# Gathering one unit's u with the next unit's kv and y on TensorE, from the fourth batch on

## The chip, the core and the metric

The kernel runs on one core of a Trainium2 chip. The metric is the device time of one launch in microseconds. One launch does everything below; inputs and output lie in the chip's memory.

## The reference, cut to what matters

```
# q, k, v: (8, 8, 576, 64)
q_s  = softmax(q, over the 64 columns)        k_s = softmax(k, over the 576 rows)
kv   = einsum('bhsd,bhse->bhde', k_s, v)      attn = einsum('bhsd,bhde->bhse', q_s, kv)
x    = attn as (8, 576, 512)
h    = relu(x^T @ w_tok1) @ w_tok2            # 576 -> 256 -> 576, over the rows
u    = x + h^T
out  = u + relu(u @ w_ch1) @ w_ch2            # 512 -> 1536 -> 512, over the columns
```

## The kernel before

The work has two kinds of pieces.

**Units.** A unit is one batch `b` and one pair of heads `j`; there are 8 x 4 = 32 of them, `n = 4 b + j`. A unit goes through these steps on TensorE:
- `softmax_k` holds one small product (L235, 128 columns, full fp32, two passes: "mb"), which spreads the maxima of k over the partitions.
- `stage_kv` makes kv: ten products of 65 columns in full fp32 (L277). The trace counts two passes for each, 20 rows.
- `stage_y` makes y = q_s^T w_tok1: 14 products of 256 columns (L337). Its operands are split into a high and a low part of type fp32r.
- `stage_h1` multiplies y by kv: two products of 128 columns in full fp32 (L345, four passes) and splits the result into `hh` and `hl`.
- `stage_u` makes u in two parts of 320 and 256 columns, nine fp32r products each (L381). Its results are copied into `uh` by ScalarE (L388) and `ul` by VectorE (L389).
- `stage_qT` turns q on VectorE and ScalarE (L315, L323) and splits it into `qth`, `qtl`, which `stage_u` reads. It has no product here.

**Steps.** The channel product runs over 9 groups `g` of 512 rows and 12 slices `f`. A step `(g, f)` is `ch1` (L409, 12 products of 512 columns into one `ps_h` bank, emptied by ScalarE L412 and VectorE L413 into `h2h`, `h2l`), and then `ch2` of the step before (L421, 12 products of 512 columns into the four `ps_o` banks). After a group's last `ch2`, `out_end` empties `ps_o` (L452, L453).

`todo` says where unit pieces go: an entry at `i` is issued in step `i` between its `ch1` and the `ch2`, an entry at `i + 0.5` after that `ch2`. A step is 24 products of 512 columns. `n0` = 24 is the first step of group 2; groups begin at `n0`, `n0 + 12` and so on. From the fourth batch on, unit `n` has its entries at `n0 + 12 (b - 3) + 3 j`, so that four units go with one group of 12 steps.

All pieces of later units and all `ch1` share the four `ps_h` banks, in turn. `qh`, `ql`, `qth`, `qtl`, `ys`, `hh`, `hl`, `kvh`, `kvl` have one buffer each. The order on an engine is not the order in which the code issues: a scheduler places instructions by its own estimate, within the dependences. An engine then runs its list in that order.

Of the kernel before, what the change touches and what calls it, by code (L numbers as in the profile page):

```python
# [20 lines left out]
def attn_mixer_kernel(ctx: ExitStack, tc: tile.TileContext, q, k, kt, v, wt, out, dims):  # L21
# [6 lines left out]
    NF = DCH // P  # L28
# [80 lines left out]
    def f32(ap):  # L109
        return ap.bitcast(F32)  # L110

    def split(hi, lo, src, lo_eng):

        nc.scalar.copy(hi, src)  # L114
        lo_eng.tensor_tensor(lo, src, f32(hi), op=ALU.subtract)  # L115
# [3 lines left out]
    def ps_unit(dtype=F32):  # L119

        pools = unit_banks[0]
        pool, name = pools[turn[0] % len(pools)]
        turn[0] += 1
        return pool.tile([P, 512], dtype, name=name)
# [25 lines left out]
    def load_v(n):  # L150
        if n < NU and n not in v_of:
            t = v_ring[n % 2 if n < NE else 0]
            for h in range(2):
                nc.sync.dma_start(t[:, 0:C, h, 0:D], v[n][:, 0:C, h * D : (h + 1) * D])
            nc.sync.dma_start(t[0:TL, C, :, 0:D], v[n][0:TL, C, :].rearrange("p (h d) -> p h d", h=2))
            v_of[n] = t
# [113 lines left out]
    def stage_kv(u):  # L270
        kx, vt = u["k"], v_of[u["n"]]
        kv = ps_unit()

        for c in range(C1):
            for h in range(2):
                hs = slice(h * D, (h + 1) * D)
                nc.tensor.matmul(kv[hs, 0 : D + 1], kx[:, c, hs], vt[:, c, h, :], start=(c == 0), stop=(c == C))  # L277

        if u["n"] != NE - 1:
            load_v(u["n"] + 2 if u["n"] < NE else u["n"] + 1)  # L280
        rs = sm.tile([P, 1], F32, name="rs")
        nc.vector.tensor_scalar(rs, kv[:, D : D + 1], 1e-9, None, op0=ALU.add)
        nc.vector.reciprocal(rs, rs)
        kvf = kv_ring[u["n"] % len(kv_ring)]
        for h in range(2):
            hs = slice(h * D, (h + 1) * D)
            nc.scalar.activation(kvf[hs, hs], kv[hs, 0:D], AF.Copy, scale=rs[hs])
        u["kvf"] = kvf
        if u["early"]:
            return  # L290
        kvh = wk.tile([P, P], F32R, name="kvh")
        kvl = wk.tile([P, P], F32R, name="kvl")
        split(kvh, kvl, kvf, nc.vector)
        u["kvh"], u["kvl"] = kvh, kvl

    def stage_qT(u):

        qx = u["q"]
        if u["early"]:
            qt = early.tile([P, S], F32, name="qt")  # L300
            t = ps_unit()
            for c in range(C):
                nc.tensor.transpose(t[:, c * P : (c + 1) * P], qx[:, c, :], f32(ident))
            nc.scalar.copy(qt[:, 0:S0], t)
            t = ps_unit()
            nc.tensor.transpose(t[:, 0:P], qx[:, C, :], f32(ident))
            nc.scalar.copy(qt[:, S0:S], t[:, 0:TL])
            u["qt"] = qt
            return
        qth = wk.tile([P, S], F32R, name="qth")  # L310
        qtl = wk.tile([P, S], F32R, name="qtl")
        u["qth"], u["qtl"] = qth, qtl

        turned = cv.tile([P, C1 * P], U32, name="cv_s").bitcast(F32).rearrange("p (c t) -> p c t", t=P)
        nc.vector.transpose(turned, qx)  # L315
        k = 0
        for x in range(P // Q):
            n = C1 if x * Q < TL else C
            for y in range(P // Q):
                xs, ys = slice(x * Q, (x + 1) * Q), slice(y * Q, (y + 1) * Q)  # L320
                eng = (nc.vector.tensor_copy, nc.vector.tensor_copy, nc.scalar.copy)[k % 3]
                k += 1
                eng(qx[ys, 0:n, xs], turned[xs, 0:n, ys])  # L323
        split(qth, qtl, qx.rearrange("p c t -> p (c t)")[:, 0:S], nc.vector)

    def stage_y(u):
        y = ps_unit()
        if u["early"]:
            mm = [(u["q"][:, c, :], w1f[:, c, :]) for c in range(C1)]
        else:  # L330
            qh, ql = u["qh"], u["ql"]
            mm = []
            for c in range(C):
                mm += [(qh[:, c, :], w1h[:, c, :]), (qh[:, c, :], w1l[:, c, :]), (ql[:, c, :], w1h[:, c, :])]
            mm += [(qh[:, C, :], w1th), (qh[:, C, :], w1tl)]
        for i, (a, w) in enumerate(mm):
            nc.tensor.matmul(y[:, 0:TOK], a, w, start=(i == 0), stop=(i == len(mm) - 1))  # L337
        ys = (early if u["early"] else wk).tile([P, TOK], F32, name="ys")
        nc.scalar.copy(ys, y[:, 0:TOK])
        u["y"] = ys  # L340

    def stage_h1(u):
        h1 = ps_unit()
        for n in range(NT):
            nc.tensor.matmul(  # L345
                h1[:, n * P : (n + 1) * P], u["y"][:, n * P : (n + 1) * P], u["kvf"], start=True, stop=True
            )
        pool = early if u["early"] else wk
        hh = pool.tile([P, NT, P], F32R, name="hh")
        hl = pool.tile([P, NT, P], F32R, name="hl")  # L350
        src = h1[:, 0 : NT * P].rearrange("p (n c) -> p n c", n=NT)
        nc.scalar.activation(hh, src, AF.Relu)
        nc.vector.scalar_tensor_tensor(hl, src, 0.0, f32(hh), op0=ALU.max, op1=ALU.subtract)  # L353
        u["hh"], u["hl"] = hh, hl
# [7 lines left out]
    def stage_u(u, half):  # L362
        b, j = u["b"], u["j"]
        edge = (b + 1) * CW - b * S
        cut = min(max(edge, S - 320), 320)
        n0, n1 = ((0, cut), (cut, S))[half]
        N = n1 - n0
        ns = slice(n0, n1)
        t = ps_unit()
        if u["early"]:  # L370
            mm = [(u["kvf"], u["qt"][:, ns])]
        else:
            mm = [(u["kvh"], u["qth"][:, ns]), (u["kvh"], u["qtl"][:, ns]), (u["kvl"], u["qth"][:, ns])]
        for n in range(NT):
            mm += [
                (u["hh"][:, n, :], w2h[:, n, ns]),
                (u["hh"][:, n, :], w2l[:, n, ns]),
                (u["hl"][:, n, :], w2h[:, n, ns]),
            ]
        for i, (a, w) in enumerate(mm):  # L380
            nc.tensor.matmul(t[:, 0:N], a, w, start=(i == 0), stop=(i == len(mm) - 1))  # L381
        for g, a0, a1 in ((b, n0, min(n1, edge)), (b + 1, max(n0, edge), n1)):
            if a0 < a1:
                at = b * S + a0 - g * CW
                uh, ul = (x[:, j, at : at + a1 - a0] for x in uT[g])
                src = t[:, a0 - n0 : a1 - n0]
                emptied[:] = [
                    nc.scalar.copy(uh, src).ins,  # L388
                    nc.vector.tensor_tensor(ul, src, f32(uh), op=ALU.subtract).ins,  # L389
                ]  # L390
# [66 lines left out]
    units = {}  # L457

    def begin(n):
        if n < NU and n not in units:  # L460
            units[n] = load_unit(n // NJ, n % NJ)

    def soft(n):
        if n < NU:
            softmax_k(units[n])
            softmax_q(units[n])

    def pe_stages(n):
        def s1():
            stage_qT(units[n])  # L470
            stage_kv(units[n])

        def s2():
            stage_y(units[n])

        def s3():
            stage_h1(units[n])
            stage_u(units[n], 0)

        def s4():  # L480
            stage_u(units[n], 1)

        return s1, s2, s3, s4
# [64 lines left out]
    n0 = len(steps)  # L548
# [9 lines left out]
    def put(at, fn):  # L558
        todo.setdefault(int(2 * at) / 2, []).append(fn)

    put(n0 - 12, prepare)
    for n in range(NE, NU):
        b, j = divmod(n, NJ)
        if b == 2:
            at = (n0 - 10, n0 - 9, n0 - 9, n0 - 7.5) if j == 0 else [n0 - 9.5 + 2 * j + x for x in (0, 0.5, 1, 1.5)]
        else:
            at = [n0 + (b - 3) * NF + 3 * j + x for x in (0, 1, 1.5, 2)]
        s1, s2, s3, s4 = pe_stages(n)
        put(at[0], s1)
        put(at[0], lambda n=n: soft(n + 1))  # L570
        put(at[0] + 0.5, lambda n=n: begin(n + 2))
        for x, fn in zip(at[1:], (s2, s3, s4)):
            put(x, fn)

    pend = None

# [84 lines left out]
```

## Time and profile before

| | |
|---|---|
| median of 3 runs | 822.23 us (821.69 to 822.65) |
| profiled execution | 822.09 us, of which the span of the engines is 820.3 |
| TensorE busy | 803.5 us, 98% of the span |
| VectorE, ScalarE, GpSimd busy | 490.5, 340.0, 84.4 us |
| TensorE's waits that the trace names | 10.7 us, all before 239 us |

The first 180 us prepare weights and the first two batches; units of the third batch end at 231 us. From 239 us to 682 us the 20 units of batches four to eight run among the steps, and from 682 us on only steps are left. In the timeline a row gives the start, the time, the engine, the line, the operation, and how many like it follow one another ("x2"). The times of single matrix products overlap: what one costs is the distance from its start to the next start.

### The profile page before, as it was taken

What the parts mean: (1) busy time and instruction counts of PE and PEld (TensorE: products, weight loads), DVE (VectorE), ACT (ScalarE), POOL (GpSimd) and SP (SyncE); (2) the same over time, 40 slices, a digit from 0 to 9 for tenths busy, and PEclk for the clock granted to TensorE, in tenths of its full rate; (3) what the DMA queues carried; (4) which work ended last, traced back from release to release, by engine and by line L of the source; (5) the groups of instructions that cost most, each with busy time, mean ns of one, the idle gap of its engine ahead of it and who ended that gap; (6) DMA issues with size and microseconds to landing.
All of it is one profiled execution on the core that took longest, in us unless ns stands there. A gap on an engine that the chain in (4) does not pass through costs nothing.

```text
span 820.3 us, 11946 instructions
## 1 busy us (share of the span) xinstructions
PE 803.5 (98%) x4512; PEld 678.1 (83%) x4512; DVE 490.5 (60%) x1104; ACT 340.0 (41%) x898; POOL 84.4 (10%) x69
## 2 busy tenths in 40 slices
PE   7899999989999999999999999999999999999997
PEld 6688888878888888888888888888888888888886
DVE  6999998897875455855576555845575324113112
ACT  6976564457544344443434443434443421101110
POOL 1000010102201011111111111101111100000100
PEclk9999999999999999999999999999999999999999
DMA  9753433424222112312232221312121001001001
GB/s 298 241 161 93 150 108 113 139 83 126 64 73 85 48 53 63 109 52 64 64 114 63 64 64 35 113 47 63 39 91 48 15 1 51 1 1 51 1 1 51
DMA packets 60634, 63.55 MB, mean 77 GB/s; under 512 B 40865, under 2 KB 40993, under 8 KB 60577
## 3 DMA queue, kind: packets, MB, share of 16 engines
q1 hardware_dynamic: 55392, 53.36, 22.2%
q10 hardware_dynamic: 5184, 9.44, 3.1%
q8 instruction: 35, 0.57, 0.3%
q14 instruction: 23, 0.18, 0.1%
HBM read 53.35 MB, written 9.44 MB: 77 GB/s over the span
## 4 chain that ended last, share of the span: by engine, by line
PE 89%; DVE 6%; DMA 3%; ACT 1%; SPq 1%; issue 0%; DVEq 0%; ACTq 0%
PE ps_h L409 34%; PE ps_o L421 34%; PE ps_h L381 8%; PE ps_h L337 5%; PE ps_h L277 2%; DMA stg<-in_w 2%; PE ps_h L345 1%; DMA kt_t<-in_kt 1%; PE ps_o L381 1%; PE ps_h L235 1%; PE ps_o L337 1%; DVE mc L219 1%; DVE q_t L323 1%; DVE cv_s L176 1%; DVE cv_s L181 1%; DVE stg L179 0%
## 5 line engine op out<-in xcount | busy, mean ns | idle before, releaser
L409 PE MATMUL ps_h<-uh,cw 128*128 128x512 f32 x864 | 268.6, 391 | 0.3 <-DVE cw L115 0.3
L421 PE MATMUL ps_o<-h2h,cw 128*128 128x512 f32 x864 | 250.0, 392 | 2.2 <-DVE cw L115 2.2
L421 PEld LDWEIGHTS ps_o<-h2h,cw 128*128 128x128 f32 x864 | 160.0, 188 | 34.7 <-ACT h2h L412 2.4
L409 PEld LDWEIGHTS ps_h<-uh,cw 128*128 128x128 f32 x864 | 159.3, 188 | 31.6 <-DVE cw L115 0.8
L413 DVE SCALAR_TENSOR_TENSOR h2l<-ps_h,h2h 128x512 fp32r<-128x512 f32 x108 | 74.3, 688 | 170.4 <-ACT h2h L412 170.2
L412 ACT ACTIVATE h2h<-ps_h 128x512 fp32r<-128x512 f32 x108 | 64.4, 596 | 253.8 <-PE ps_h L409 251.5
L409 PE MATMUL ps_h<-ul,cw 128*128 128x512 f32 x432 | 168.7, 390 | 0.0
L421 PE MATMUL ps_o<-h2l,cw 128*128 128x512 f32 x432 | 151.9, 394 | 0.0
L409 PEld LDWEIGHTS ps_h<-ul,cw 128*128 128x128 f32 x432 | 81.1, 188 | 17.4
L421 PEld LDWEIGHTS ps_o<-h2l,cw 128*128 128x128 f32 x432 | 79.7, 188 | 15.9
L323 DVE COPY q_t<-cv_s 32x160 f32<-32x160 f32 (+1 forms) x264 | 62.1, 235 | 45.2 <-POOL ql L115 41.9
L237 POOL TENSOR_TENSOR k_t<-k_t,mb 128x640 f32<-128x640 f32 x24 | 38.0, 1583 | 350.6 <-ACT mb L236 350.6
L115 POOL TENSOR_TENSOR ql<-q_t,qh 128x640 fp32r<-128x640 f32 x24 | 39.2, 1633 | 220.7 <-ACT qh L114 218.2
L245 DVE TENSOR_REDUCE st<-q_t 128x10 f32<-128x640 f32 x32 | 26.2, 817 | 38.2 <-DMA q_t<-in_q 38.2
L323 ACT COPY q_t<-cv_s 32x128 f32<-32x128 f32 (+1 forms) x120 | 36.8, 307 | 2.1 <-DVE cv_s L315 0.7
L256 ACT ACTIVATE q_t<-q_t 128x640 f32<-128x640 f32 x24 | 17.7, 739 | 40.4 <-DVE q_t L255 40.4
L381 PE MATMUL ps_h<-w2h,hh 128*128 128x256 f32 (+1 forms) x112 | 32.6, 299 | 0.0
L381 PE MATMUL ps_h<-w2l,hh 128*128 128x256 f32 (+1 forms) x112 | 32.6, 296 | 0.0
L389 DVE TENSOR_TENSOR ul<-ps_h,uh 128x320 fp32r<-128x320 f32 (+4 forms) x76 | 26.8, 372 | 7.4 <-ACT uh L388 6.8
L388 ACT CAST uh<-ps_h 128x320 fp32r<-128x320 f32 (+4 forms) x76 | 24.4, 337 | 15.6 <-PE ps_h L381 11.2
L381 PE MATMUL ps_h<-w2h,hl 128*128 128x320 f32 (+1 forms) x112 | 29.8, 300 | 0.3 <-DVE hl L353 0.2
L219 DVE TENSOR_REDUCE mc<-kt_t 128x1 f32<-128x640 f32 x32 | 25.9, 809 | 4.8 <-DMA kt_t<-in_kt 3.5
(144 smaller groups left out, 1077.8 us busy)
## 6 DMA issues: line engine op xcount, KB each, us to landing
stg<-in_w SPq DMA_DIRECT2D x28, 512.0 KB, 4.0
kt_t<-in_kt SPq DMA_DIRECT2D x32, 320.0 KB, 3.2
q_t<-in_q SPq DMA_DIRECT2D x32, 320.0 KB, 3.1
v_t<-in_v SPq DMA_DIRECT2D x64, 128.0 KB, 2.6
out<-stg ACTq DMA_DIRECT2D x32, 256.0 KB, 2.1
k_t<-in_k SPq DMA_DIRECT2D x24, 320.0 KB, 3.3
v_t<-in_v SPq DMA_DIRECT2D x32, 32.0 KB, 2.5
out<-part ACTq DMA_DIRECT2D x4, 256.0 KB, 2.3
```

The costliest lines, as they stand in the source:

```text
L115: lo_eng.tensor_tensor(lo, src, f32(hi), op=ALU.subtract)
L219: nc.vector.tensor_reduce(mc, ktt, axis=AX.X, op=ALU.max)
L237: nc.gpsimd.tensor_tensor(kx, kx, mb.unsqueeze(1).broadcast_to([P, C1, P]), op=ALU.subtract)
L245: nc.vector.tensor_reduce(st[:, 0, :], qt, axis=AX.X, op=ALU.max)
L323: eng(qx[ys, 0:n, xs], turned[xs, 0:n, ys])
L337: nc.tensor.matmul(y[:, 0:TOK], a, w, start=(i == 0), stop=(i == len(mm) - 1))
L381: nc.tensor.matmul(t[:, 0:N], a, w, start=(i == 0), stop=(i == len(mm) - 1))
L389: nc.vector.tensor_tensor(ul, src, f32(uh), op=ALU.subtract).ins,
L409: nc.tensor.matmul(t, cw[f][x][:, n, :], w, start=(i == 0), stop=(i == 3 * NJ - 1))
L412: nc.scalar.activation(hh, t, AF.Relu).ins,
L413: nc.vector.scalar_tensor_tensor(hl, t, 0.0, f32(hh), op0=ALU.max, op1=ALU.subtract).ins,
L421: nc.tensor.matmul(o, cw[f][x][:, n, :], w, start=(first and i == 0), stop=(last and i == 2))
```

## The change

Before, the entries of a unit from the fourth batch on were: qT and kv at `at`, y at `at + 1`, h1 and half of u at `at + 1.5`, the other half at `at + 2`. Now they are gathered. At `at - 1` come both halves of u of the unit before, then kv, y and qT of this unit; h1 follows at `at + 0.5`, and u of the last unit stands alone. `at - 1` is step 2, 5, 8 or 11 of a group's 12, where `at` was 0, 3, 6 or 9. The softmax of the next unit and the loads of the one after keep their places behind kv (now also behind y).

```diff
+    prev = None
     for n in range(NE, NU):
         b, j = divmod(n, NJ)
+        s1, s2, s3, s4 = pe_stages(n)
         if b == 2:
             at = (n0 - 10, n0 - 9, n0 - 9, n0 - 7.5) if j == 0 else [n0 - 9.5 + 2 * j + x for x in (0, 0.5, 1, 1.5)]
-        else:
-            at = [n0 + (b - 3) * NF + 3 * j + x for x in (0, 1, 1.5, 2)]
-        s1, s2, s3, s4 = pe_stages(n)
-        put(at[0], s1)
-        put(at[0], lambda n=n: soft(n + 1))
-        put(at[0] + 0.5, lambda n=n: begin(n + 2))
-        for x, fn in zip(at[1:], (s2, s3, s4)):
-            put(x, fn)
+            put(at[0], s1)
...
+            continue
+        at = n0 + (b - 3) * NF + 3 * j - 1
+        if prev is not None:
+            put(at, lambda n=prev: (stage_u(units[n], 0), stage_u(units[n], 1)))
+        put(at, lambda n=n: (stage_kv(units[n]), stage_y(units[n]), stage_qT(units[n])))
+        put(at, lambda n=n: soft(n + 1))
+        put(at + 0.5, lambda n=n: begin(n + 2))
+        put(at + 1.5, lambda n=n: stage_h1(units[n]))
+        prev = n
+    put(at + 3, lambda n=prev: (stage_u(units[n], 0), stage_u(units[n], 1)))
```

In the lists of instructions below, a number behind a name tells buffers apart, and "x2" stands for so many alike in a row. TensorE before, where group 3 begins and unit 16 has its kv:

```order
L421 MATMUL ps_o<-h2h_109,cw_1388 128x512 x7
L277 MATMUL ps_h<-v_t,k_t 64x65 x2
L409 MATMUL ps_h<-uh_101,cw_117 128x512 x2
L277 MATMUL ps_h<-v_t,k_t 64x65
L409 MATMUL ps_h<-ul_105,cw_117 128x512
L277 MATMUL ps_h<-v_t,k_t 64x65 x7
L235 MATMUL ps_h<-dg,ones 128x128
L421 MATMUL ps_o<-h2l_113,cw_1388 128x512 x3
L421 MATMUL ps_o<-h2h_109,cw_1388 128x512
L421 MATMUL ps_o<-h2l_113,cw_1388 128x512
L409 MATMUL ps_h<-uh_101,cw_117 128x512 x2
```

The kv products stand in three pieces, with `ch1` products (L409) of the next group between them, and mb (L235) directly behind. Four units, the first ones of the last four batches, have kv in three pieces like this; the other sixteen have it in one. TensorE now, the end of u of unit 15, kv of unit 16 and the beginning of its y:

```order
L381 MATMUL ps_h<-w2h,hh 128x256
L381 MATMUL ps_h<-w2l,hh 128x256
L381 MATMUL ps_h<-w2h,hl 128x256
L277 MATMUL ps_h<-v_t,k_t 64x65 x10
L337 MATMUL ps_h<-w1h,qh 128x256
L337 MATMUL ps_h<-w1l,qh 128x256
L337 MATMUL ps_h<-w1h,ql 128x256
```

And the end of that y:

```order
L337 MATMUL ps_h<-w1h,ql 128x256
L337 MATMUL ps_h<-w1th,qh 128x256
L337 MATMUL ps_h<-w1tl,qh 128x256
L235 MATMUL ps_h<-dg,ones 128x128
L421 MATMUL ps_o<-h2h_108,cw_1388 128x512 x2
L421 MATMUL ps_o<-h2l_112,cw_1388 128x512
```

kv is whole in all 20 units. u, kv and y follow each other with nothing between them. mb comes directly behind y in units 13 to 20, as in unit 12, and six or seven `ch2` products later in units 21 to 30. Behind h1 no half of u follows any more, but products of 512 columns.

VectorE before, around u of unit 19 and kv of unit 20 (h2l is the second half of an emptied `ch1` tile, qtl belongs to unit 20, `rs` is the sum in kv, L452 begins the emptying of `ps_o`):

```order
L353 SCALAR_TENSOR_TENSOR hl<-ps_h,hh 128x256
L413 SCALAR_TENSOR_TENSOR h2l_113<-ps_h,h2h_109 128x512
L115 TENSOR_TENSOR qtl<-q_t,qth 128x576
L389 TENSOR_TENSOR ul_104<-ps_h,uh_100 128x256
L389 TENSOR_TENSOR ul_106<-ps_h,uh_102 128x320
L245 TENSOR_REDUCE st<-q_t 128x10
L255 TENSOR_TENSOR q_t<-q_t,st 128x640
L257 TENSOR_REDUCE st<-q_t 128x10
L282 TENSOR_SCALAR rs<-ps_h 128x1
L413 SCALAR_TENSOR_TENSOR h2l_112<-ps_h,h2h_108 128x512
L452 TENSOR_TENSOR stg<-ps_o,uh_101 128x512
```

VectorE now, around the gathered place of u of unit 19 and kv of unit 20:

```order
L315 STREAM_TRANSPOSE cv_s<-q_t 128x640
L413 SCALAR_TENSOR_TENSOR h2l_112<-ps_h,h2h_108 128x512
L413 SCALAR_TENSOR_TENSOR h2l_113<-ps_h,h2h_109 128x512
L389 TENSOR_TENSOR ul_104<-ps_h,uh_100 128x256
L115 TENSOR_TENSOR qtl<-q_t,qth 128x576
L389 TENSOR_TENSOR ul_106<-ps_h,uh_102 128x320
L282 TENSOR_SCALAR rs<-ps_h 128x1
L283 RECIPROCAL rs<-rs 128x1
L115 TENSOR_TENSOR kvl<-kvf_110,kvh 128x128
L219 TENSOR_REDUCE mc<-kt_t 128x1
```

Two `ch1` tiles are emptied one after the other ahead of the u tiles, and the sum and the reciprocal of kv (L282, L283) and `kvl` (L115) follow directly, where the first row of kv stood behind three rows of softmax (L245, L255, L257).

More of the change, by code (lines that the diff above doesn't have):

```diff
@@ L561, in attn_mixer_kernel @@
     put(n0 - 12, prepare)
+    prev = None
     for n in range(NE, NU):
         b, j = divmod(n, NJ)
+        s1, s2, s3, s4 = pe_stages(n)
         if b == 2:
             at = (n0 - 10, n0 - 9, n0 - 9, n0 - 7.5) if j == 0 else [n0 - 9.5 + 2 * j + x for x in (0, 0.5, 1, 1.5)]
-        else:
-            at = [n0 + (b - 3) * NF + 3 * j + x for x in (0, 1, 1.5, 2)]
-        s1, s2, s3, s4 = pe_stages(n)
-        put(at[0], s1)
-        put(at[0], lambda n=n: soft(n + 1))
-        put(at[0] + 0.5, lambda n=n: begin(n + 2))
-        for x, fn in zip(at[1:], (s2, s3, s4)):
-            put(x, fn)
+            put(at[0], s1)
+            put(at[0], lambda n=n: soft(n + 1))
+            put(at[0] + 0.5, lambda n=n: begin(n + 2))
+            for x, fn in zip(at[1:], (s2, s3, s4)):
+                put(x, fn)
+            continue
[8 more added lines that the diff above has]
+    put(at + 3, lambda n=prev: (stage_u(units[n], 0), stage_u(units[n], 1)))
     pend = None
```

## The prediction

> **What bounds the kernel now.** I read the busy times first, then TensorE's waits, then its timeline unit by unit.
>
> ```profile
> span 820.3 us, 11946 instructions
> PE 803.5 (98%) x4512; PEld 678.1 (83%) x4512; DVE 490.5 (60%) x1104; ACT 340.0 (41%) x898; POOL 84.4 (10%) x69
> ```
>
> TensorE is busy for 98% of the span. Since a busy row may hide a stall (the ends of products are modelled), I looked at its waits:
>
> ```profile
> PE ps_h L226 <- ACT kt_t L223: 2.5, 2, 1.9
> ...
> PE ps_h L381 <- DVE hl L353: 0.2, 1, 0.2
> ```
>
> The ten rows of that view come to 10.7 us, and cut to the time from 239 us on the same view is empty. From there TensorE waits for nothing, which the stretch of one batch, from the first kv to that of the next, says as well:
>
> ```profile
> 328.38:417.69 89.31, 89.31 (x522) 75.52 (x521) 54.30 (x125) 36.79 (x88) 12.57 (x8) 1.00 0.25 70
> ```
>
> It is 89.31 us long and TensorE is busy in all of it; VectorE is busy for 54 us and ScalarE for 37. What decides there is how many start-to-start distances TensorE strings together and how long each is. In the part without units:
>
> ```profile
> 698.01 0.61 PE L409 MATMUL ps_h<-uh,cw 128*128 128x512 f32 x2
> ...
> 700.73 0.61 PE L421 MATMUL ps_o<-h2h,cw 128*128 128x512 f32 x2
> ```
>
> Twelve products of 512 columns take 2.72 us, 0.2267 each. A batch has 12 steps x 24 = 288 of them, 65.28 us. The other 24.03 us belong to four units. I read the price of a piece thus: from a 512-wide start ahead of it to the second one or so behind it, less 0.2267 for each 512-wide start in between.
>
> **What a unit costs now.** A whole kv with its mb:
>
> ```profile
> 350.11 0.39 PE L409 MATMUL ps_h<-ul,cw 128*128 128x512 f32 x1
> 350.42 0.80 PE L277 MATMUL ps_h<-v_t,k_t 128*64 128x65 f32 x20
> 351.15 0.49 PE L235 MATMUL ps_h<-dg,ones 128*128 128x128 f32 x2
> 351.40 0.71 PE L421 MATMUL ps_o<-h2h,cw 128*128 128x512 f32 x2
> 351.95 0.39 PE L421 MATMUL ps_o<-h2l,cw 128*128 128x512 f32 x1
> ```
>
> From 350.11 to 351.95 are 1.84 us; three starts of 512 columns lie in it (one at 350.11, two at 351.40): 1.84 - 0.68 = 1.16. kv in three pieces:
>
> ```profile
> 327.60 0.84 PE L421 MATMUL ps_o<-h2h,cw 128*128 128x512 f32 x3
> 328.38 0.34 PE L277 MATMUL ps_h<-v_t,k_t 128*64 128x65 f32 x4
> 328.64 0.73 PE L409 MATMUL ps_h<-uh,cw 128*128 128x512 f32 x2
> 329.30 0.33 PE L277 MATMUL ps_h<-v_t,k_t 128*64 128x65 f32 x2
> 329.56 0.50 PE L409 MATMUL ps_h<-ul,cw 128*128 128x512 f32 x1
> 329.99 0.68 PE L277 MATMUL ps_h<-v_t,k_t 128*64 128x65 f32 x14
> ...
> 330.85 0.95 PE L421 MATMUL ps_o<-h2l,cw 128*128 128x512 f32 x3
> 331.63 0.39 PE L421 MATMUL ps_o<-h2h,cw 128*128 128x512 f32 x1
> ```
>
> From 327.60 to 331.63 are 4.03 us with nine such starts (3, 2, 1, 3): 4.03 - 2.04 = 1.99. The same 20 passes and the same mb cost 0.83 us more, though nobody waited: each way into kv and out of it has a price. Then y, h1 with half of u, and the rest of u:
>
> ```profile
> 356.73 0.39 PE L409 MATMUL ps_h<-ul,cw 128*128 128x512 f32 x1
> 356.96 0.28 PE L337 MATMUL ps_h<-w1h,qh 128*128 128x256 f32 x1
> ...
> 358.63 0.64 PE L421 MATMUL ps_o<-h2h,cw 128*128 128x512 f32 x2
> 359.11 0.39 PE L421 MATMUL ps_o<-h2l,cw 128*128 128x512 f32 x1
> ```
>
> ```profile
> 363.90 0.39 PE L421 MATMUL ps_o<-h2l,cw 128*128 128x512 f32 x1
> 364.12 0.61 PE L345 MATMUL ps_h<-kvf,ys 128*128 128x128 f32 x4
> ...
> 364.92 0.63 PE L409 MATMUL ps_h<-uh,cw 128*128 128x512 f32 x2
> 365.39 0.39 PE L409 MATMUL ps_h<-ul,cw 128*128 128x512 f32 x1
> ```
>
> ```profile
> 367.44 0.39 PE L409 MATMUL ps_h<-ul,cw 128*128 128x512 f32 x1
> 367.67 0.30 PE L381 MATMUL ps_h<-qth,kvh 128*128 128x320 f32 x1
> ...
> 369.71 0.63 PE L409 MATMUL ps_h<-uh,cw 128*128 128x512 f32 x2
> 370.17 0.39 PE L409 MATMUL ps_h<-ul,cw 128*128 128x512 f32 x1
> ```
>
> y: 359.11 - 356.73 = 2.38, less three starts: 1.70. h1 with half of u: 365.39 - 363.90 = 1.49, less three: 0.81. The rest of u: 370.17 - 367.44 = 2.73, less three: 2.05. A unit is 1.16 + 1.70 + 0.81 + 2.05 = 5.72; four of them and 0.83 make 23.71. To 24.03 lack 0.32, or 0.02 for each of the 16 places where narrow products end: behind each the next dozen 512-wide ones start some 0.23 apart and not 0.2267.
>
> **The change, part by part.** The ways in and out can be read where the third batch already has u and kv in one block:
>
> ```profile
> 214.01 0.28 PE L381 MATMUL ps_h<-w2h,hl 128*128 128x256 f32 x1
> 214.22 0.80 PE L277 MATMUL ps_h<-v_t,k_t 128*64 128x65 f32 x20
> 214.95 0.50 PE L421 MATMUL ps_o<-h2h,cw 128*128 128x512 f32 x1
> 215.29 0.38 PE L235 MATMUL ps_h<-dg,ones 128*128 128x128 f32 x2
> 215.43 0.48 PE L421 MATMUL ps_o<-h2h,cw 128*128 128x512 f32 x1
> 215.74 0.39 PE L421 MATMUL ps_o<-h2l,cw 128*128 128x512 f32 x1
> ```
>
> - *Into kv.* From u: 214.22 - 214.01 = 0.21, where a product of 256 columns takes 0.12 (y: 1.67 for 14), so 0.09. From 512 columns: 350.42 - 350.11 = 0.31 against 0.23, also about 0.09. Gathering changes nothing.
> - *Out of kv.* Into 512 columns: 215.29 - 214.95 = 0.34, so 0.11 more than usual. No row of units like these shows kv followed by an fp32r y. Bounds: 0, if the narrower product hides it, and 0.20, what the step from 329.56 to 329.99 (0.43) has over 0.23 where a way out meets a way in. I take 0.11, the row nearest to it, the same as today: no change. The ends are worth 19 x 0.11 = -2.1 and 19 x 0.09 = +1.7 us.
> - *mb behind y.* Standing behind a 512-wide product it costs (215.74 - 215.29) - 0.2267 = 0.22; in kv with mb today it is about as much. No change; if it is apart from y, it has an end of its own, 0.02 to 0.05.
> - *The four split kv become whole.* 4 x 0.83 = 3.3 us. That is the main term. What now stands at a group's beginning are `ch1` and `ch2` products in turn, all 512 wide, whose change costs nothing: at 700.73 `ch2` follows `ch1` at the plain distance.
> - *Fewer ends.* A unit had four ends of narrow products (kv with mb, y, half of u, the rest of u). Now it has two (the gathered place, h1) in units 13 to 20, and three in units 21 to 30, where mb stands apart. h1 itself goes on paying for its way out, now into 512 columns. An end is 0.02 by the sum above, up to 0.05 if all its slow starts are counted. Eight units gain two ends, ten gain one: 26 x 0.02 = 0.5 us, less a little for mb, 0.4.
> - *Moved work off TensorE.* qT, the softmax, the loads and the copies out of PSUM are as many as before, on engines that are busy for 61% and 41% of a batch. On SP's queue v of the next unit now goes ahead of q; q has to wait for the turned copy in any case, and is needed a unit later. GpSimd's two passes for a unit change places (ql now ahead of the shift of k); GpSimd is busy for 12.57 us of a batch, and the shifted k is needed by the next unit's kv only. What hides all this is TensorE's 22 us from unit to unit; where that cover fails is the second rival.
>
> Sum: -3.3 - 0.4 = -3.7 us against the profiled execution of 822.09, which lies 0.14 under the median of the runs, 822.23. That gives 818.4.
>
> The Trainium skill ("TensorE: Matmul & The Clock Gate", Back-to-back issue gap) gives the distance between products from the number of columns alone, N / 2.4 + 2.5 ns; for 512 columns that is 216 ns as an estimate from that page, and the rows above have 227. By such a rule the order of products is free and the sum of this change would be nothing. The rows of the split kv speak against it.
>
> **Rivals.**
> - *The order of products costs nothing, or the gaps in the split kv move elsewhere: no change, 822.1.* It would be so if 1.99 against 1.16 came from operands that arrived late and still do. For it: the split stands only at a group's beginning, where much goes on. Against: the waits name nothing there, and the added distances, 0.43 and 0.34, are those of other ways in and out of kv. It is what the rule of that page would make of the time.
> - *The gathered place runs out of `ps_h` banks: slower.* It takes banks for u, u, kv and y in a row behind a `ch1` tile. y takes the bank of that tile, so it waits for VectorE's L413, and all that is behind it in TensorE's list waits too.
>
> ```profile
> 361.29 2.73 DVE L323 COPY q_t<-cv_s 32x160 f32<-32x160 f32 x11 [2.81 <-POOL ql L115]
> ...
> 368.50 0.69 DVE L413 SCALAR_TENSOR_TENSOR h2l<-ps_h,h2h 128x512 fp32r<-128x512 f32 x1 [2.89 <-ACT h2h L412]
> ```
>
> The `ch1` of 367.44 ends at about 367.83 and its bank is free at 369.19, 1.4 us later. All of u (from 367.67 to 369.71 are 2.04 for 15 of its 18 products, and 3 x 0.12 more: 2.4) and kv (0.8) give 3.2 us: a reserve of 1.8. It is gone if the 2.73 us of copies (361.29) come just when `ch1` ends: 2.73 + 0.69 = 3.4, a wait of 0.2 in y. From 0.19 us in each of 19 places (3.7 / 19) the gain is gone; with a transposition of 0.85 more in front, it would be 1.1 each, 21 us, 839. Against: in the list of VectorE the copies stand behind kv's rows, and L413 ahead of u's. At half a microsecond each it would be 818.4 + 9.5 = 828. The Trainium skill says likewise ("PSUM — Partial Sum Buffer", Engine vs sequencer instructions) that matmuls start and complete in program order; the trace of before cannot show such a wait, having none here.
> - *Part of the gain goes into waits:* at the five beginnings of a group, `ps_o` must be emptied with no kv or y in between to cover it. 0.2 to 0.4 each, 1 to 2 us: 819.4 to 820.4.
>
> **How the numbers follow.** Forecast 0.79; partial gain 0.08; no change 0.08; slower 0.05. The forecast's own range is 817.6 to 819.2. Half of each bound of kv's way out into y, -1.1 and +0.9, and up to 0.5 for mb's own ends, widen it to 817.2 and 819.8, which leaves out the no-change and slower cases and the last part of partial gain. A measurement of this kernel can tell about 0.2%, 1.6 us, so faster is below 820.6: 0.79 + 0.08 = 0.87. Within 0.2% is 0.08, slower 0.05.
>
> **What would show it.** In the trace after, kv (L277) is one row of 20 in all 20 units, with no 512-wide start within. A batch, from one first kv to the next, is 65.28 + 4 x 5.76 = 88.3 us early on, near 88.5 in the last batches, where it was 89.31. The first y product starts 0.22 before the second. TensorE's waits stay empty behind 239 us; a row of L337 waiting for L413, or of L421 waiting for L452, would be the second or third rival. A batch of 89.3 with whole kv would refute the price of ways in and out.

## The result, and the profile after

The changed kernel takes 816.97 us (median of 6 runs, 815.83 to 817.88), the kernel before 822.0 in runs beside it: a ratio of 0.9936, with an interval of 0.9921 to 0.9952. It is faster, as forecast, and by more than forecast: 5.0 us and not 3.7, which puts it 0.2 us below the stated range.

The first lines of the page after, and the three stretches from the first kv of a batch to that of the next (in such a row: the stretch, its length, the busy time of TensorE and of its weight loads, of VectorE, ScalarE and GpSimd, the granted clock, the DMA share and GB/s):

```profile
span 816.1 us, 11997 instructions
PE 797.1 (98%) x4512; PEld 677.0 (83%) x4512; DVE 486.7 (60%) x1104; ACT 342.2 (42%) x898; POOL 83.6 (10%) x69
```

```profile
322.72:410.70 87.98, 87.98 (x521) 75.53 (x521) 53.43 (x125) 37.28 (x89) 12.38 (x8) 1.00 0.23 71
410.70:498.75 88.05, 88.05 (x521) 75.53 (x520) 52.99 (x128) 37.80 (x92) 12.40 (x8) 1.00 0.24 71
498.75:586.91 88.16, 88.16 (x521) 75.54 (x520) 52.74 (x129) 37.75 (x93) 12.36 (x8) 1.00 0.23 67
```

TensorE is still the bound and its waits behind 239 us are still none: the view is empty, as before. A batch of 89.31 us has become one of 87.98 to 88.16, and TensorE is busy in all of it. So nothing was filled up; the start-to-start distances that it strings together got shorter. The profiled execution is at 817.88, 4.21 under the profiled 822.09. Two pairs of rows from TensorE's timeline, of before and then of after, show where that lies (h1 of unit 11, the last piece ahead of the changed order, and the last row of products):

```profile
225.20 0.60 PE L345 MATMUL ps_h<-kvf,ys 128*128 128x128 f32 x4
...
814.06 1.07 PE L421 MATMUL ps_o<-h2l,cw 128*128 128x512 f32 x4
```

```profile
226.30 0.60 PE L345 MATMUL ps_h<-kvf,ys 128*128 128x128 f32 x4
...
809.87 1.07 PE L421 MATMUL ps_o<-h2l,cw 128*128 128x512 f32 x4
```

From the one to the other are 588.86 us before and 583.57 after: 5.29 us were won where the change is, and 1.1 us were lost in the first 225 us, where TensorE's order is the same in both. The loss is a matter of TensorE's granted clock. One and the same stretch, before and then after:

```profile
171.90:175.30 3.40, 3.40 (x20) 2.94 (x19) 2.16 (x4) 1.93 (x7) 1.36 (x1) 1.00 0.32 96
```

```profile
171.90:175.30 3.40, 3.40 (x10) 2.66 (x9) 0.98 (x3) 1.82 (x6) 1.20 (x1) 0.50 0.34 96
```

At a granted clock of 0.50 instead of 1.00 TensorE gets through 10 instructions and not 20. The same 12 products of 512 columns take 2.84 us before (171.23 to 174.07) and 4.42 after (171.09 to 175.51), which is more than the whole loss. Of the runs below, `y_apart`, `u_apart` and `kv_wide` have such a stretch near there too, the others don't; behind it the clock is 1.00 up to the last product in all of them. In the kernels of this study the first part ended anywhere from 224.4 to 228.7 us. Comparisons below therefore go by the part behind h1 of unit 11, which I call the body, and by the stretches.

The gathered place in the timeline of after:

```profile
364.02 0.39 PE L409 MATMUL ps_h<-ul,cw 128*128 128x512 f32 x1
364.25 0.28 PE L381 MATMUL ps_h<-qth,kvh 128*128 128x256 f32 x1
...
366.48 0.31 PE L381 MATMUL ps_h<-w2h,hl 128*128 128x320 f32 x1
366.71 0.80 PE L277 MATMUL ps_h<-v_t,k_t 128*64 128x65 f32 x20
367.45 0.38 PE L337 MATMUL ps_h<-w1h,qh 128*128 128x256 f32 x1
367.67 0.28 PE L337 MATMUL ps_h<-w1l,qh 128*128 128x256 f32 x1
...
369.09 0.28 PE L337 MATMUL ps_h<-w1tl,qh 128*128 128x256 f32 x1
369.20 0.38 PE L235 MATMUL ps_h<-dg,ones 128*128 128x128 f32 x2
369.34 0.71 PE L421 MATMUL ps_o<-h2h,cw 128*128 128x512 f32 x2
369.89 0.39 PE L421 MATMUL ps_o<-h2l,cw 128*128 128x512 f32 x1
...
371.95 0.39 PE L421 MATMUL ps_o<-h2l,cw 128*128 128x512 f32 x1
```

First u ends (L381), then come the 20 passes of kv (L277), the 14 products of y (L337), mb (L235) and `ch2`. kv is one row of 20 in all 20 units. From 366.48 to 366.71 are 0.239 us (by the unrounded starts), 0.09 more than the 0.147 of a 320-wide product: the way into kv. The first y product starts 0.223 ahead of the second, the others 0.118 apart: the way out is 0.105.

Full prices of pieces are needed for what follows. I took them as the prediction did, but up to the 12th or 14th 512-wide start behind the piece, so that its slow starts are in. For the gathered place that is from 364.02 to 371.95, 7.93 us, less 12 x 0.2267: 5.214 by the unrounded starts. A unit of before is kv with mb 1.187, y 1.727, h1 with the first three products of u 0.827 and the other 15 of u 2.060, together 5.801 us. A unit of after is the gathered place 5.214 and h1 0.460, together 5.674; where mb stands apart (0.255 to 0.272 beside 4.985 to 4.994), 5.70 to 5.73. And 65.28 + 4 x 5.674 = 87.98 is the first stretch above. So the gain is 0.81 for each of four split kv, 3.25 us, and 0.127 or some 0.09 for each of the units, about 1.9 us; the body shows 5.29.

### The profile page after: what moved, and what is told of

It is laid out like the page before. It is cut to its first block, busy times and chain, and to the rows that moved or that the text cites. A ratio compares the mean times of both kernels' runs of the same rounds, so it can differ in the third digit from the quotient of the medians.

```text
span 816.1 us, 11997 instructions
## 1 busy us (share of the span) xinstructions
PE 797.1 (98%) x4512; PEld 677.0 (83%) x4512; DVE 486.7 (60%) x1104; ACT 342.2 (42%) x898; POOL 83.6 (10%) x69
## 4 chain that ended last, share of the span: by engine, by line
PE 89%; DVE 6%; DMA 3%; ACT 1%; issue 1%; DVEq 0%; ACTq 0%
PE ps_h L409 34%; PE ps_o L421 34%; PE ps_h L381 8%; PE ps_h L337 6%; PE ps_h L277 2%; DMA stg<-in_w 2%; PE ps_h L345 1%; PE ps_o L381 1%; DVE mc L219 1%; PE ps_h L235 1%; DVE cv_s L176 1%; DVE q_t L323 1%; DMA q_t<-in_q 1%; DVE st L245 1%; ACT q_t L251 1%
## 5 line engine op out<-in xcount | busy, mean ns | idle before, releaser
L409 PE MATMUL ps_h<-uh,cw 128*128 128x512 f32 x864 | 269.7, 392 | 0.6 <-DVE cw L115 0.6
L421 PE MATMUL ps_o<-h2h,cw 128*128 128x512 f32 x864 | 263.4, 394 | 2.2 <-DVE cw L115 2.2
L409 PEld LDWEIGHTS ps_h<-uh,cw 128*128 128x128 f32 x864 | 160.3, 188 | 33.2 <-DVE cw L115 1.0
L413 DVE SCALAR_TENSOR_TENSOR h2l<-ps_h,h2h 128x512 fp32r<-128x512 f32 x108 | 74.0, 685 | 187.3 <-ACT h2h L412 186.9
L409 PE MATMUL ps_h<-ul,cw 128*128 128x512 f32 x432 | 168.2, 389 | 0.0
L421 PE MATMUL ps_o<-h2l,cw 128*128 128x512 f32 x432 | 161.7, 392 | 0.0
L421 PEld LDWEIGHTS ps_o<-h2l,cw 128*128 128x128 f32 x432 | 81.4, 189 | 16.8
L409 PEld LDWEIGHTS ps_h<-ul,cw 128*128 128x128 f32 x432 | 81.1, 188 | 17.0
L115 POOL TENSOR_TENSOR ql<-q_t,qh 128x640 fp32r<-128x640 f32 x24 | 39.3, 1636 | 484.8 <-ACT qh L114 406.3
L323 DVE COPY q_t<-cv_s 32x160 f32<-32x160 f32 (+1 forms) x264 | 65.8, 249 | 6.3 <-POOL ql L115 3.0
L245 DVE TENSOR_REDUCE st<-q_t 128x10 f32<-128x640 f32 x32 | 26.2, 818 | 41.8 <-DMA q_t<-in_q 41.8
L381 PE MATMUL ps_h<-w2h,hh 128*128 128x320 f32 (+1 forms) x112 | 33.4, 299 | 0.0
L381 PE MATMUL ps_h<-w2l,hh 128*128 128x320 f32 (+1 forms) x112 | 33.0, 296 | 0.0
L381 PE MATMUL ps_h<-w2h,hl 128*128 128x320 f32 (+1 forms) x112 | 32.7, 298 | 0.0
L389 DVE TENSOR_TENSOR ul<-ps_h,uh 128x320 fp32r<-128x320 f32 (+4 forms) x76 | 27.2, 373 | 4.0 <-ACT uh L388 3.1
```

The source lines that it names most:

```text
L245: nc.vector.tensor_reduce(st[:, 0, :], qt, axis=AX.X, op=ALU.max)
L409: nc.tensor.matmul(t, cw[f][x][:, n, :], w, start=(i == 0), stop=(i == 3 * NJ - 1))
L413: nc.vector.scalar_tensor_tensor(hl, t, 0.0, f32(hh), op0=ALU.max, op1=ALU.subtract).ins,
L421: nc.tensor.matmul(o, cw[f][x][:, n, :], w, start=(first and i == 0), stop=(last and i == 2))
```

## The experiments

The forecast had the ends of narrow products at 0.02 us each and their saving at 0.4 us in all. Three theories were on the table. By A every way into and out of kv has its price, so that whole kv alone brings 3.3 us, and the joining of pieces brings the rest. By B the gain comes from where the pieces stand in a group. By C the split of kv costs nothing by itself, and the gathering brings all. The verdict of each run is a ratio to the kernel before, timed beside it (823.09 us for the first four, 823.52 for the last three). Edits are cut to what matters and stand against the changed kernel, the first one against the kernel before; where an edit adds lines, the line numbers in the rows move with it.

**Only the place: `shift`.** The pieces of before, each one step earlier, nothing gathered.

```diff
-            at = [n0 + (b - 3) * NF + 3 * j + x for x in (0, 1, 1.5, 2)]
+            at = [n0 + (b - 3) * NF + 3 * j - 1 + x for x in (0, 1, 1.5, 2)]
```

> The pieces of a unit stay apart as before (kv with mb, y, h1 with half of u, the rest of u); only their places move one step earlier, so that none begins a group. In TensorE's list kv is whole in all 20 units. Theory A (each way into and out of kv costs about 0.4 us together, and ends of narrow products cost the rest): the four split kv become whole, 4 x 0.83 = 3.3 us less than before and nothing more, a batch of 88.5 us against 89.31, about 818.8 us. Rival B (the gain of the changed kernel is from where the pieces stand in a group, not from gathering): all of it is here, 5 us, about 817, a batch of 88.0. Rival C (the split costs nothing by itself, the gathering brings all): no change from before, 822, a batch of 89.3.

819.19 us, ratio 0.9954 (0.9940 to 0.9969). The stretch of the same batch:

```profile
323.05:411.58 88.53, 88.53 (x522) 75.38 (x521) 55.09 (x125) 36.80 (x88) 12.57 (x8) 1.00 0.24 71
```

kv is whole in all 20 units, the batch is 0.78 shorter than before, and the body 3.0 us shorter. That is the term of the split kv, which the forecast had at 3.3, shown by itself: the step that begins no group is worth it without any gathering. B would have had all of the gain here, a batch of 88.0, and C none of it, 89.3; the batch is the 88.5 of A. It is also the end of the prediction's first rival: the same instructions in a shorter time with no wait in either. (The Trainium skill, "TensorE: Matmul & The Clock Gate", Back-to-back issue gap, has a formula for the isolated distance between products that goes by the number of columns alone; by it this kernel would have stayed at 822, and the run does not agree.) What is left of the 5.29, over 2 us, belongs to the gathering.

**y out of the gathered place: `y_apart`.**

```diff
-        put(at, lambda n=n: (stage_kv(units[n]), stage_y(units[n]), stage_qT(units[n])))
+        put(at, lambda n=n: (stage_kv(units[n]), stage_qT(units[n])))
+        put(at + 1, lambda n=n: stage_y(units[n]))
```

> Gathered as in the changed kernel, but y comes one step later, alone; u, kv and mb stay together. Theory A with ends sized from the changed kernel's trace (behind y 0.05 us, behind u 0.025, behind kv with mb 0.03, behind h1 0.01, and y itself 0.02 faster behind kv): a unit of 5.75 us instead of 5.67 to 5.73, 0.02 to 0.08 more, about 1.0 us more in all than the changed kernel, 818.0. The forecast's size of an end (0.02 each): 0.4 more, 817.4. Rival B (place alone): no difference from the changed kernel, 817.0.

819.31 us, ratio 0.9952 (0.9938 to 0.9965). The stretch, and how y ends here:

```profile
324.31:412.62 88.31, 88.31 (x521) 75.63 (x520) 58.81 (x125) 36.96 (x89) 12.59 (x8) 1.00 0.23 71
```

```profile
376.58 0.28 PE L337 MATMUL ps_h<-w1tl,qh 128*128 128x256 f32 x1
376.70 0.64 PE L421 MATMUL ps_o<-h2h,cw 128*128 128x512 f32 x2
377.17 0.39 PE L421 MATMUL ps_o<-h2l,cw 128*128 128x512 f32 x1
...
379.24 0.39 PE L421 MATMUL ps_o<-h2l,cw 128*128 128x512 f32 x1
379.47 0.39 PE L421 MATMUL ps_o<-h2h,cw 128*128 128x512 f32 x1
```

The batch is 0.33 longer than after, and the body 1.2 us. By the prices of the pieces (3.560 for u with kv and mb, 1.727 for y) it is 0.074 for a unit; one unit of the batch also has u in two pieces, for 0.03 us. The second fence shows more than half of the 0.074: from 376.70 to 379.47 are 12 distances in 2.77 us, where 12 x 0.2267 are 2.72. y has an end of 0.05 us when 512-wide products follow it, two and a half times what the forecast gave to any end. The other part is put down to pace: its 14 products take 1.673 us here and before (0.1196 each), and behind kv 13 distances from 367.67 to 369.20 take 1.53 (0.118 each).

**u out of the gathered place: `u_apart`.**

```diff
-            put(at, lambda n=prev: (stage_u(units[n], 0), stage_u(units[n], 1)))
+            put(at - 0.5, lambda n=prev: (stage_u(units[n], 0), stage_u(units[n], 1)))
```

> Gathered as in the changed kernel, but u of the unit before comes half a step earlier, so that the 12 products of ch1 lie between it and kv; mb is directly behind y in all units. Theory A: u by itself 2.40 us, kv with y and mb 2.84, h1 0.46, together 5.70, the mean of what the changed kernel has (5.67 with mb at y, 5.73 with mb apart): no difference that can be measured, 817.0, a batch of 88.1. If u behind 512 columns and kv behind u shared some cost that the gathering saves (0.09 for the way in): 20 x 0.09 = 1.8 more, 818.8.

818.27 us, ratio 0.9939 (0.9926 to 0.9952). Two stretches, and the one row of TensorE's waits from 240 us on:

```profile
321.90:410.05 88.15, 88.15 (x522) 75.24 (x521) 55.32 (x124) 36.72 (x88) 12.44 (x8) 1.00 0.25 71
498.37:587.73 89.36, 88.19 (x522) 75.21 (x521) 55.06 (x128) 36.99 (x92) 12.43 (x8) 1.00 0.23 65
```

```profile
PE ps_h L337 <- DVE ul L389: 1.2, 1, 1.2
```

The undisturbed batch is 0.17 longer than after: u alone 2.400, kv with y and mb 2.840, h1 0.460, a unit of 5.700. So u next to kv saves 0.026; the rest of the 0.17 is one u that stands in three pieces, 2.46 in all. The body is 1.67 us longer, and 1.2 of that is one wait, in the batch of the second row (89.36 long, TensorE busy for 88.19): y of one unit stood at 522.42 behind a `ps_h` bank that VectorE was still emptying of u. That is the mechanism of the second rival (its releaser there was L413, here L389), once in 20 units, where u had been cut and pushed to a group's beginning. All TensorE work behind y waited with it (which is what the Trainium skill says in "PSUM — Partial Sum Buffer", Engine vs sequencer instructions: matmuls start and complete in program order). The changed kernel has u whole and never meets it.

**One way into kv more: `kv_cut`.** The last two of kv's five pairs come half a step later.

```diff
...
-        put(at, lambda n=n: (stage_kv(units[n]), stage_y(units[n]), stage_qT(units[n])))
+        put(at, lambda n=n: (stage_kv(units[n], 0), stage_y(units[n]), stage_qT(units[n])))
+        put(at + 0.5, lambda n=n: stage_kv(units[n], 1))
```

> As the changed kernel, but in each of the 20 units the last two of kv's five pairs of products come half a step later, between ch2 and the next ch1. One more way in and out for each unit, nothing else. Theory A: 0.41 us each (half of the 0.83 that two cuts cost in a split kv), 20 x 0.41 = 8.1 us more than the changed kernel, 825. Rival B, and rival C, by which cutting has no price of its own: within 0.5 us of the changed kernel, 817.

825.16 us, ratio 1.0026 (1.0017 to 1.0035): slower than before. A stretch, and the pieces of one kv:

```profile
323.64:413.22 89.58, 89.58 (x522) 75.55 (x521) 56.17 (x125) 36.95 (x89) 14.63 (x8) 1.00 0.23 70
```

```profile
368.42 0.57 PE L278 MATMUL ps_h<-v_t,k_t 128*64 128x65 f32 x12
368.92 0.74 PE L424 MATMUL ps_o<-h2h,cw 128*128 128x512 f32 x2
369.50 0.40 PE L424 MATMUL ps_o<-h2l,cw 128*128 128x512 f32 x1
...
370.20 0.28 PE L340 MATMUL ps_h<-w1h,qh 128*128 128x256 f32 x1
...
373.45 0.39 PE L424 MATMUL ps_o<-h2l,cw 128*128 128x512 f32 x1
373.77 0.45 PE L278 MATMUL ps_h<-v_t,k_t 128*64 128x65 f32 x8
374.15 0.73 PE L412 MATMUL ps_h<-uh,cw 128*128 128x512 f32 x2
374.72 0.39 PE L412 MATMUL ps_h<-ul,cw 128*128 128x512 f32 x1
```

The batch is 1.60 longer than after, 0.40 for a unit; the body is 8.24 longer. But the cut is not alone: the scheduler put some `ch2` products between the first 12 passes (368.42) and y (370.20), so y has lost its neighbour here too. Beside `y_apart`, which has y apart and kv whole, a unit costs 6.08 against 5.75: 0.33 for one more visit to kv. In the split kv of before two more visits cost 0.81. In the rows the visit is seen: 0.32 from 373.45 to 373.77 on the way in (0.09 more than the plain distance), and 0.57 for the first two 512-wide starts on the way out, 0.12 more than plain. A third part lies inside: from the first pass to the start behind the last, 8 passes take 0.38 (373.77 to 374.15), 12 take 0.50 (368.42 to 368.92) and 20 in the changed kernel 0.74. That is 0.03 for a pass and some 0.14 that each visit pays once.

**The old place, with kv and y gathered: `group_start`.** Places 0, 3, 6 and 9 as before; both halves of u issued together, two steps later.

```diff
-        at = n0 + (b - 3) * NF + 3 * j - 1
...
+        at = n0 + (b - 3) * NF + 3 * j
...
+        put(at + 2, lambda n=n: (stage_u(units[n], 0), stage_u(units[n], 1)))
```

> kv and y of a unit gathered at the old places (steps 0, 3, 6, 9 of a group, so that one of four begins a group), u of the same unit in one place two steps later, h1 as before. In TensorE's list kv is whole in 19 of the 20 units and cut once in the other. Theory A (only what stands next to what counts): from the blocks measured so far kv with y and mb 2.84, h1 0.46, u in three pieces about 2.45, 5.75 a unit and 0.41 once, 4.1 us less than before in the time from the third batch's end, ratio 0.995. Rival B (a step that begins a group is the wrong place in itself): at most the 2 us of the gathering, ratio 0.9975, and waits of TensorE at the beginnings of groups.

819.25 us, ratio 0.9945 (0.9933 to 0.9957). A batch whose kv are all whole:

```profile
415.38:503.67 88.29, 88.29 (x521) 75.23 (x520) 58.08 (x128) 37.55 (x93) 12.89 (x8) 1.00 0.25 71
```

kv is whole in 19 units and cut in one; the body is 3.65 us shorter than before. So a step that begins a group does not by itself cut kv or make anything wait. Before, the order chosen by the scheduler cut it there in four units; with y put directly behind it, it did so in one. The cut kv:

```profile
325.94 0.33 PE L277 MATMUL ps_h<-v_t,k_t 128*64 128x65 f32 x2
326.20 0.72 PE L409 MATMUL ps_h<-uh,cw 128*128 128x512 f32 x2
326.76 0.40 PE L409 MATMUL ps_h<-ul,cw 128*128 128x512 f32 x1
327.09 0.80 PE L277 MATMUL ps_h<-v_t,k_t 128*64 128x65 f32 x18
```

The price of that cut is read in its pieces: 3.31 for kv with y and mb instead of 2.84, so 0.47 for the second visit, where one of the ten products had been split from the others. The whole kv at the beginning of a group, as at 415.38, cost the same 2.84 as elsewhere. What the batch has over the 87.98 of after, 0.31, is u apart from kv, u in two pieces in every unit (2.43 to 2.45 instead of 2.40) and h1 in two pieces in one unit (0.52 instead of 0.46).

**Is it the shape of kv? `kv_wide`.** From unit 8 on kv is five products of 128 x 130, both heads at once, instead of ten of 64 x 65; the blocks that mix heads are not used.

```diff
...
+            for c in range(C1):
+                both = vt[:, c, :, :].rearrange("p h d -> p (h d)")
+                nc.tensor.matmul(kv[:, 0 : 2 * D + 2], kx[:, c, :], both, start=(c == 0), stop=(c == C))
```

> As the changed kernel, but kv of units 8 to 31 is five products of 128 columns of weights and 130 columns of the other operand, for both heads at once, of which only the two blocks on the diagonal are used; the same output. Full fp32 as before, two passes each. It asks what the way into and out of kv hangs on. Theory W (on the 64-column shape of its weights: h1 and mb are full fp32 too and cost no more than their passes): no longer distance in front of kv or behind it; ten passes of 130 columns at about 0.111, 1.11 us where kv costs 0.93 with its ways in and out, 24 x 0.18 = 4 us more than the changed kernel. Theory F (on the change between full fp32 and fp32r): the ways stay, 0.2 on top of 1.11, 24 x 0.38 = 9 us more.

825.49 us, ratio 1.0023 (1.0012 to 1.0035). A stretch, and one kv:

```profile
325.76:414.62 88.86, 88.86 (x483) 77.39 (x481) 58.00 (x129) 36.93 (x89) 13.79 (x8) 1.00 0.24 70
```

```profile
370.02 0.31 PE L389 MATMUL ps_h<-w2h,hl 128*128 128x320 f32 x1
370.17 1.28 PE L282 MATMUL ps_h<-v_t,k_t 128*128 128x130 f32 x10
371.20 0.71 PE L429 MATMUL ps_o<-h2h,cw 128*128 128x512 f32 x2
371.75 0.39 PE L429 MATMUL ps_o<-h2l,cw 128*128 128x512 f32 x1
```

From 370.02 to 370.17 are 0.146 us, the plain distance of a 320-wide product: with products of 128 weight columns and 130 others the way in is gone, though kv is still full fp32 between fp32r products. On the way out the two 512-wide starts take 0.55, 0.10 over the plain 0.45, as h1 does (0.55 from 377.98 to 378.53 in the rows further down); that belongs to the last fp32 pass. A pass is then (1.03 + 0.10) / 10 = 0.11, and u with kv costs 3.507 here against some 3.35 in `y_apart` (3.560 less about 0.21 for mb): 0.16 more. Ten passes of 0.11 instead of twenty in 0.74 would be 0.39 more; the ways in and out that vanish, 0.09 and 0.105, account for 0.20 of the difference of 0.23. So the way in hangs on the shape of kv's products and not on the change of type. The run changes two things at once, the weight columns (64 to 128) and the columns of the other operand (65 to 130); which of them it is, was not tried. The profiled span is 6.4 us longer than after's: 4.0 in the body, and 2.4 before it, since h1 of unit 11 starts at 228.72 here and not at 226.30. Of these 2.4, 1.6 are one wait of TensorE for ScalarE, at 209.00, which the changed kernel does not have:

```profile
PE ps_o L429 <- ACT h2h L420: 1.6, 1, 1.6
```

Against the kernel before, the whole time lies about 7 us above the changed kernel's, between the 4 of theory W and the 9 of theory F, so it does not decide. The body does: 4.0 us over 20 units are 0.20 for a unit, where W had 0.18 and F 0.38. In this kernel, as in the cut one, `ch2` products stand between kv and y, so that y's lost neighbour is in the 0.20 as well.

**h1 also in the gathered place: `one_place`.**

```diff
+            put(at, lambda n=prev: stage_h1(units[n]))
+        put(at, lambda n=n: (stage_kv(units[n]), stage_y(units[n])))
...
-        put(at + 1.5, lambda n=n: stage_h1(units[n]))
```

> As the changed kernel, but h1 of the unit before joins the gathered place too: h1 of one unit, kv and y of the next, u of the one before. In TensorE's list seven products of 512 columns lie between y and u, and mb is directly behind u in all units. Theory A from the blocks measured: h1 with kv and y 0.44 + 2.63 = 3.07, u 2.40, mb 0.21, together 5.68 a unit where the changed kernel has 5.67 (mb at y) and 5.71 to 5.73 (mb apart): 0.3 to 0.6 us less than the changed kernel, which cannot be told by the time. Rival (u behind h1 with only kv and y between waits for hh or hl, or kv's copies wait for u and hold up ScalarE): 0.2 to 0.5 us in each unit, 4 to 10 us more.

817.24 us, ratio 0.9922 (0.9909 to 0.9934). A stretch:

```profile
320.06:408.12 88.06, 88.06 (x522) 75.71 (x521) 54.47 (x124) 37.04 (x89) 13.53 (x8) 1.00 0.25 71
```

A unit is 5.69 (h1 with kv and y 3.053, u with mb 2.640, with some `ch2` products between them), the batch 0.08 longer than the same one of after, the body 0.18 shorter. By time the two cannot be told apart. h1 has next to nothing to save, which the changed kernel shows as well, h1 between 512-wide products:

```profile
377.39 0.39 PE L421 MATMUL ps_o<-h2l,cw 128*128 128x512 f32 x1
377.62 0.60 PE L345 MATMUL ps_h<-kvf,ys 128*128 128x128 f32 x4
377.98 0.71 PE L409 MATMUL ps_h<-uh,cw 128*128 128x512 f32 x2
378.53 0.39 PE L409 MATMUL ps_h<-ul,cw 128*128 128x512 f32 x1
378.76 0.39 PE L409 MATMUL ps_h<-uh,cw 128*128 128x512 f32 x1
```

From 377.39 to 378.76 are 1.37 us with four 512-wide distances: 0.46, of which its four passes of 0.109 are 0.44. No run of the study beat the changed kernel by more than can be measured.

## Why the prediction was right or wrong

- *TensorE is bound and waits for nothing* from 239 us on: right, before and after, with the clock at 1.00 in every stretch. The ten rows of its earlier waits come to 11.3 us, not 10.7; they all lie before 239 us, so nothing rests on it.
- *The four split kv become whole, -3.3 us*: right. 0.81 each by the full prices, 3.25; `shift` shows 3.0 with nothing else gathered.
- *Into kv, 0.09, no change*: right (0.239 against 0.147). *Out of kv into y, taken as 0.11 between 0 and 0.20*: right, 0.105. *The first y product 0.22 ahead of the second*: 0.223.
- *mb behind y costs the same 0.22; apart 0.02 to 0.05 more*: right. It takes 0.21 behind y (5.214 less 5.007, the gathered place of the last unit, which has no mb), and 0.255 to 0.272 apart.
- *Moved work off TensorE costs nothing*: right; no wait in the changed kernel, though `u_apart` has one of 1.2 us.
- *Fewer ends, 0.4 us*: this is the step that failed. The term measured 1.9 us by the prices of units, and 2.0 as what the body shows beside the 3.25. The prediction gave 0.02 to every end, by spreading what lacked in the sum, 0.32 us, evenly over 16 places. Three things were wrong in that. Prices cut off at the second start had already swallowed a part of the slow starts. Ends differ: about 0.01 for h1, 0.025 for u, 0.05 for y, so that what the change removes is dear and what it adds (h1 before 512 columns) is cheap; "h1 itself goes on paying for its way out" was the wrong way round. And y runs at another pace behind kv. The runs give the 0.127 of a unit in three pieces: u whole instead of in two parts, one with h1, 0.027 (0.827 + 2.060 against 0.460 + 2.400); u joined to kv, 0.026 (`u_apart`); y joined to kv, 0.074 (`y_apart`), of it 0.05 its end and 0.024 its pace.
- *A batch of 88.3 early on, near 88.5 later*: 87.98 to 88.16, for the same reason. 88.31 is what `y_apart` has.
- The sum with the measured sizes, 3.25 + 1.9 = 5.2, is the body's 5.29; medians show 5.0. The upper bound that the prediction itself named for an end, 0.05, would have made its 26 ends 1.3 us and the time 817.5. The range was drawn around the lower value. Its lower end of 817.2 does not quite follow from the terms named for it, 818.4 - 1.1 = 817.3; the time lies below both.

What stays open: why slow starts of some 0.23 us follow narrow products at all, why a visit to kv pays its fixed part, and why y runs at 0.118 behind kv and at 0.1196 between 512-wide products. The end of y was shown by a run of its own; those of h1 and of a u cut in two are read from prices of pieces alone.

## What to carry to other kernels

On an engine that is full and never waits, order is still a cost: price a piece between plain starts far on both sides, a dozen or more behind it, since the products that follow it carry a part of its price. Price each kind of neighbour by itself; a remainder spread evenly over unlike places here gave a term about a fifth of its size. And when a gather is planned, look whether the pieces stay whole in the list: most of this gain came from kv not being cut, which moving the pieces by one step gave alone, and so, in 19 of 20 units, did gathering at the old places.

## What was unexpected of the hardware

- One more visit to kv's products (64 columns of weights, 65 of the other operand) costs 0.33 (`kv_cut`) to 0.47 us (`group_start`). The way in, 0.09 of it, is not there with 128 and 130 columns (`kv_wide`).
- Full-fp32 products of 128 columns (h1) between fp32r products of 512 cost little more than their four passes of 0.109: 0.46 in all.
- 256-wide y products run 1.3% closer together behind kv than between 512-wide products.
